# Attention and MoE in one kernel: masks of the first batch on VectorE, more units ahead of batch 1, weights and tokens loaded in another order

## Chip, cores, metric

The kernel runs on one core of one Trainium2 chip. The metric is the device time of one execution in microseconds (us).

In this text TensorE does the matrix multiplications (PE in the profile; PEld is its loading of weights), VectorE is DVE, ScalarE is ACT, GpSimd is POOL, and SyncE is SP, which here issues most DMAs. "Landed" means that a DMA's data has arrived.

## The reference

```python
# 8 batches, 8 heads, 576 tokens, 64 columns a head
scores = q @ k.T / sqrt(64) - slope[h] * (i - j)        # kept where 0 <= i - j < 128
attn   = softmax(scores) @ v
x = attn.transpose(0, 2, 1, 3).reshape(4608, 512)
h = x @ w_in                                            # w_in: 512 x 2048
g = h * clip(h + 3, 0, 6) / 6
out = g @ w_out                                         # w_out: 2048 x 512, out: 4608 x 512 float32
```

## The kernel before

A *group* is two heads of one batch; there are 32 of them, and group 4 opens batch 1, group 8 batch 2. Each group needs its scores (diagonal blocks in `pd`, off-diagonal ones in `po`), exponentials on ScalarE, masks on GpSimd, and the values (`av`), divided on VectorE to `avs`. The MoE part is cut into *units* of four matmuls of 128x512, and `fill(n)` puts n units where TensorE would otherwise wait. A unit needs finished batches, so there is none to put in during batch 0.

Batches 0 and 1 transpose q and k on TensorE. From batch 2 on, q and k are loaded token by token into `ldbuf`, cast by GpSimd into the one buffer `tbuf`, and transposed from there by a DMA into `qTb` and `kTb`. There is one `tbuf`, so each cast waits for the transposing DMA ahead of it. Each engine takes its instructions in the order of the program: in GpSimd's timeline below, the masks of group 9 start at 99.0 us, right behind the cast that began at 96.2.

```python
def load_weights_out():                    # 4 loads of 512 KB, issued by GpSimd
    for g in range(4):
        nc.gpsimd.dma_start(out=w_out_sb[:, ts(g, 4), :], in_=moe_w_out[...])

def load_tokens(b, nm):                    # 5 loads, issued by SyncE
    t = next_ld()[...]
    for j in range(NQ):
        nc.sync.dma_start(out=t[:n, j, :, :], in_=src_of[nm][b, ...])

def cast_tokens(b, nm):                    # q, k: GpSimd to tbuf; v: GpSimd to vbuf
    ...
def xbar(b, nm):                           # the transposing DMA, issued by SyncE
    nc.sync.dma_start_transpose(out=dst, in_=tbuf)

def exp_off(g, e):
    nc.scalar.activation(out=po[:, e], in_=sc[:, e, :], func=ACT.Exp, ...)
    nc.scalar.activation(out=p4[:, e, 0:64], ...)
    nc.gpsimd.affine_select(out=po[:, e], in_=po[:, e], ...)     # mask
    ...
def values(g, qts):                        # called with (0, 1, 2), then with (3, 4)
    av = ps_av.tile([128, 3, 2, W], FP32, tag="av", name="av")   # one PSUM buffer
    ...

def stage_next(g):                         # at the end of group g
    b, hp = divmod(g, NP)                  # NP = 4
    if g == 0:
        new_runs(1); load_runs(1, slice(0, H)); load_tokens(1, "v")
    if g == 1:
        load_weights_out()
    if b == 1:
        if hp == 1:
            load_tokens(2, "v")
        if hp in (1, 2):
            xbar(2, "qk"[hp - 1])
        if hp < 3:
            cast_tokens(2, "qkv"[hp])
    if b >= 2 and b + 1 < B:
        if hp < 2:
            xbar(b + 1, "qk"[hp])
        if hp in (0, 2):
            cast_tokens(b + 1, "kkv"[hp])
    if b >= 1 and b + 2 < B:
        if hp > 0:
            load_tokens(b + 2, "qkv"[hp - 1])
        if hp == 3:
            cast_tokens(b + 2, "q")

# main
...; load_weights_in(); first_batch()
load_tokens(2, "q"); load_tokens(2, "k")
prepare(NP); transposes(NP); prepare(NP + 1)
fill(3)
segment(NP, G, lambda g: (1, 0, 1, 0, 1, 0, 0) if g < 2 * NP else (1, 1, 1, 1, 1, 1, 2))
```

The softmax here doesn't subtract the row's maximum and nothing guards it: scores larger than these inputs give would overflow.

## Time and profile before

| | before |
|---|---|
| median time of the first three runs | 373.83 us (373.61 to 375.56) |
| span of the profiled run | 373.4 us |
| TensorE busy | 315.8 us, 85% |
| TensorE busy from 140 to 300 us | 155.3 of 160 us |
| start of scores of group 4 (batch 1) / of group 8 (batch 2) | 46.2 / 83.1 us |
| start of the cast to `tbuf` of q of batch 2 / of k of batch 3 | 54.9 / 96.2 us |
| start of values of group 9 | 104.1 us |
| from there to the end of the span | 269.3 us |

First, from the page of the kernel before, its rows of 40 equal slices of the span (9.3 us each): busy tenths of TensorE, its granted clock in tenths, busy tenths of the DMA engines, and the bandwidth.

```profile
PE   1456765666998699979999999999999999999995
PEclk9999996969999989999999999999999999999999
DMA  9999997999399959995998999531131010010012
GB/s 158 195 198 192 196 215 117 187 221 198 85 202 202 212 94 222 206 222 127 237 208 181 203 211 226 116 99 46 48 62 49 29 58 28 28 58 28 28 58 84
```

TensorE is short of work mainly in the first ten slices, and DMA is nearly full for the first 25, with three dips. So it is mainly the opening that can move the total, and two things can decide it there: TensorE's own order, or the chain of loads, casts and transposing DMAs.

The next fence is GpSimd's timeline of the kernel before: start, duration, engine, line, operation, output and input; in brackets, how long the engine had been idle and what ended it. The first line is the cast of q of batch 2, the second that of k of batch 2, the third that of k of batch 3, and the last the masks of group 9.

```profile
54.93 2.84 POOL L156 CAST tbuf<-ldbuf 128x512 bf16<-128x512 f32 x5
...
73.05 2.84 POOL L156 CAST tbuf<-ldbuf 128x512 bf16<-128x512 f32 x5 [7.70 <-issue]
...
96.22 2.83 POOL L156 CAST tbuf<-ldbuf 128x512 bf16<-128x512 f32 x5 [6.86 <-DMA qTb<-tbuf]
99.01 1.21 POOL L218 TENSOR_SCALAR_AFFINE_SELECT pd<-pd 128x512 bf16<-128x512 bf16 x2
```

The cast of k of batch 3 waits for the transposing DMA of q of batch 3, and the masks of group 9 stand behind that cast. TensorE's timeline has the scores of groups 4 and 8, and the values of group 9:

```profile
46.19 0.40 PE L195 MATMUL scd<-qTb,kTb 64*128 64x128 bf16 x8
...
83.08 0.40 PE L195 MATMUL scd<-qTb,kTb 64*128 64x128 bf16 x8
...
104.14 0.23 PE L251 MATMUL av<-vbuf,pd 128*128 128x65 bf16 x2
```

From the start of the cast at 96.2 the chain needs 2.8 us for the cast and 0.6 us for the first mask of group 9, so it would have allowed values of group 9 at 99.6 us. They start at 104.1. In the kernel before, TensorE decides, and the chain has 4.5 us to spare.

SyncE's queue in the kernel before (duration is the time to issue) shows q of batch 2 loading beside w_out, k of batch 2 after it, and the transposing DMA of k:

```profile
32.47 18.66 SPq L106 DMA_DIRECT2D ldbuf<-in_q_dram  x5
51.22 5.52 SPq L106 DMA_DIRECT2D ldbuf<-in_k_dram  x5
...
75.95 3.71 SPq L161 DMA_TRANSPOSE kTb<-tbuf  x1
```

Five loads took 18.7 us beside the weights and 5.5 us without them. The table of stretches gives, for 50 to 60 and 60 to 70 us, the busy time and count of PE, PEld, DVE, ACT and POOL, then the granted clock, the DMA share (it adds up the time of packets and can exceed 1) and GB/s:

```profile
50.00:60.00 10.00, 5.29 (x52) 3.02 (x53) 6.77 (x8) 4.79 (x10) 6.35 (x12) 0.78 1.19 206
60.00:70.00 10.00, 7.17 (x76) 4.15 (x77) 6.08 (x14) 5.79 (x12) 2.95 (x6) 0.88 0.54 101
```

### The profile page before, as it was taken

What the parts mean: (1) busy time and instruction counts of PE and PEld (TensorE: products, weight loads), DVE (VectorE), ACT (ScalarE), POOL (GpSimd) and SP (SyncE); (2) the same over time, 40 slices, a digit from 0 to 9 for tenths busy, and PEclk for the clock granted to TensorE, in tenths of its full rate; (3) what the DMA queues carried; (4) which work ended last, traced back from release to release, by engine and by line L of the source; (5) the groups of instructions that cost most, each with busy time, mean ns of one, the idle gap of its engine ahead of it and who ended that gap; (6) DMA issues with size and microseconds to landing.
All of it is one profiled execution on the core that took longest, in us unless ns stands there. A gap on an engine that the chain in (4) does not pass through costs nothing.

```text
span 373.4 us, 6509 instructions
## 1 busy us (share of the span) xinstructions
PE 315.8 (85%) x2408; PEld 160.3 (43%) x2445; DVE 174.2 (47%) x355; ACT 198.5 (53%) x361; POOL 155.3 (42%) x279
## 2 busy tenths in 40 slices
PE   1456765666998699979999999999999999999995
PEld 0334433333444345544544554455445444444442
DVE  5355456634643244545545544555445534434410
ACT  1733264545773366757776666767666343443401
POOL 7398155195555255626674762663332000000000
PEclk9999996969999989999999999999999999999999
DMA  9999997999399959995998999531131010010012
GB/s 158 195 198 192 196 215 117 187 221 198 85 202 202 212 94 222 206 222 127 237 208 181 203 211 226 116 99 46 48 62 49 29 58 28 28 58 28 28 58 84
DMA packets 153135, 51.64 MB, mean 138 GB/s; under 512 B 141200, under 2 KB 148624, under 8 KB 153104
## 3 DMA queue, kind: packets, MB, share of 16 engines
q1 hardware_dynamic: 145504, 44.54, 61.9%
q0 software_dynamic: 7456, 6.55, 10.8%
q8 instruction: 19, 0.31, 0.4%
q10 hardware_dynamic: 144, 0.13, 0.1%
q14 instruction: 12, 0.10, 0.1%
HBM read 36.70 MB, written 9.44 MB: 124 GB/s over the span
## 4 chain that ended last, share of the span: by engine, by line
PE 62%; DVE 8%; ACT 8%; issue 7%; POOL 7%; DMA 6%; SPq 1%; another core or an unknown queue 0%; POOLq 0%
PE ops L303 28%; PE hps L286 28%; ACT r L290 4%; DVE g L291 3%; DMA ldbuf<-in_v_dram 3%; DMA xT<-avs 3%; POOL pd L218 2%; ACT po L225 2%; PE av L251 2%; PE av L248 2%; PE scd L195 2%; POOL po L230 2%; DVE avs L257 1%; DVE osb L317 1%; PE sco L202 1%
## 5 line engine op out<-in xcount | busy, mean ns | idle before, releaser
L291 DVE SCALAR_TENSOR_TENSOR g<-r,hps 128x512 bf16<-128x512 f32 x144 | 99.1, 688 | 146.5 <-ACT r L290 146.4
L290 ACT ACTIVATE r<-hps,bias 128x512 f32<-128x512 f32 x144 | 99.5, 691 | 118.8 <-PE hps L286 115.4
L286 PE MATMUL hps<-xT,w_in_sb 128*128 128x512 bf16 x552 | 151.5, 390 | 11.0 <-DMA xT<-avs 5.2
L303 PE MATMUL ops<-w_out_sb,g 128*128 128x512 bf16 x563 | 144.0, 380 | 5.6 <-DVE osb L317 3.9
L303 PEld LDWEIGHTS <-g 128*128 128x128 bf16 x576 | 55.7, 98 | 78.0 <-issue 13.9
L286 PEld LDWEIGHTS <-w_in_sb 128*128 128x128 bf16 x576 | 52.5, 100 | 59.9 <-issue 11.4
L218 POOL TENSOR_SCALAR_AFFINE_SELECT pd<-pd 128x512 bf16<-128x512 bf16 x64 | 39.3, 636 | 50.3 <-ACT pd L215 50.3
L156 POOL CAST tbuf<-ldbuf 128x512 bf16<-128x512 f32 (+1 forms) x60 | 34.0, 610 | 43.1 <-issue 36.2
L230 POOL TENSOR_SCALAR_AFFINE_SELECT po<-po 128x512 bf16<-128x512 bf16 x64 | 40.0, 633 | 20.5 <-ACT po L225 17.7
L215 ACT ACTIVATE pd<-scd,bias_d 128x512 bf16<-128x512 f32 x64 | 40.7, 684 | 12.2 <-POOL pd L218 11.2
L225 ACT ACTIVATE po<-sco,bias_o 128x512 bf16<-128x512 f32 x64 | 44.1, 690 | 0.0
L248 PE MATMUL av<-vbuf,po 128*128 128x65 bf16 x256 | 27.1, 203 | 8.2 <-DVE avs L257 6.2
L251 PE MATMUL av<-vbuf,pd 128*128 128x65 bf16 x256 | 27.0, 205 | 7.2 <-POOL pd L218 7.2
L257 DVE TENSOR_TENSOR avs<-av,rc 128x384 bf16<-128x384 f32 x64 | 31.4, 491 | 2.2
L251 PEld LDWEIGHTS <-pd 128*128 128x128 bf16 x256 | 21.2, 104 | 17.6 <-POOL pd L218 8.2
L248 PEld LDWEIGHTS <-po 128*128 128x128 bf16 x256 | 20.8, 104 | 14.4 <-DVE avs L257 9.2
L256 DVE RECIPROCAL rc<-av 128x6 f32<-128x6 f32 x64 | 11.8, 184 | 23.6 <-PE av L251 23.4
L183 PE MATMUL tp<-ident,pr 96*128 96x96 bf16 x96 | 8.8, 255 | 16.1 <-DVE pr L171 10.4
L315 ACT COPY osb<-ops 128x512 f32<-128x512 f32 x18 | 10.5, 585 | 19.3 <-PE ops L303 19.3
L228 ACT ACTIVATE p4buf<-sco,bias_d 128x64 bf16<-128x64 f32 x64 | 20.7, 324 | 0.0
L317 DVE COPY osb<-ops 128x512 f32<-128x512 f32 x17 | 11.6, 684 | 7.4 <-PE ops L303 7.4
L195 PE MATMUL scd<-qTb,kTb 64*128 64x128 bf16 x256 | 13.6, 229 | 1.8 <-DVE kTb L185 1.0
(45 smaller groups left out, 150.1 us busy)
## 6 DMA issues: line engine op xcount, KB each, us to landing
out_dram<-osb SPq DMA_DIRECT2D x35, 256.0 KB, 2.3
ldbuf<-in_v_dram SPq DMA_DIRECT2D x32, 256.0 KB, 4.9
ldbuf<-in_q_dram SPq DMA_DIRECT2D x24, 256.0 KB, 4.7
ldbuf<-in_k_dram SPq DMA_DIRECT2D x24, 256.0 KB, 5.0
w_in_sb<-in_moe_w_in_dram POOLq DMA_DIRECT2D x4, 512.0 KB, 14.0
w_out_sb<-in_moe_w_out_dram POOLq DMA_DIRECT2D x4, 512.0 KB, 16.3
ldbuf<-in_v_dram SPq DMA_DIRECT2D x8, 128.0 KB, 4.7
ldbuf<-in_q_dram SPq DMA_DIRECT2D x6, 128.0 KB, 4.7
```

The lines of the kernel that those rows point to most:

```text
L156: nc.gpsimd.tensor_copy(out=tbuf[:m, :, j, :], in_=s[:m, j, :, :].rearrange("p (i e) d -> p i (e d)", e=2))
L215: nc.scalar.activation(out=pd[:, e, :, :].rearrange("p j c -> p (j c)"), in_=sc[:, e, :], func=ACT.Exp, bias=bias_d[:, h:h + 1], scale=scale)
L218: nc.gpsimd.affine_select(out=pd[:, e, :, :], in_=pd[:, e, :, :], pattern=[[0, 4], [1, 128]], channel_multiplier=-1, base=0, compare_op=AL ...
L225: nc.scalar.activation(out=po[:, e, :, :].rearrange("p j c -> p (j c)"), in_=sc[:, e, :], func=ACT.Exp, bias=bias_o[:, h:h + 1], scale=scale)
L230: nc.gpsimd.affine_select(out=po[:, e, :, :], in_=po[:, e, :, :], pattern=[[0, 4], [-1, 128]], channel_multiplier=1, base=-1, compare_op=A ...
L248: nc.tensor.matmul(av[:, i, e, :], lhsT=po[:, e, qt - 1, :], rhs=vb[:, qt - 1, h, :], start=True, stop=False)
L251: nc.tensor.matmul(av[:, i, e, :], lhsT=d, rhs=vb[:, qt, h, :], start=(qt == 0), stop=True)
L257: nc.vector.tensor_tensor(out=st[g, "avs"][:, qts[0]:qts[0] + nq, :, :], in0=av[:, 0:nq, :, 0:D], in1=rc[:, 0:nq, :, :].to_broadcast([128, ...
L286: nc.tensor.matmul(hps, lhsT=w_in_sb[:, ks, ts(ms, 128)], rhs=xT[:, ks, ts(nt, NT)], start=(ks == 0), stop=(ks == n_ks - 1))
L290: nc.scalar.activation(out=r6, in_=hps, func=ACT.Relu, bias=bias3[:, 0:1], scale=1.0 / 6.0)
L291: nc.vector.scalar_tensor_tensor(out=gts[nt][:, ms, :], in0=r6, scalar=1.0, in1=hps, op0=ALU.min, op1=ALU.mult)
L303: nc.tensor.matmul(ops[nt, sub], lhsT=gts[nt][:, ms, ts(sub, 128)], rhs=w_out_sb[:, ms, :], start=(ms == 0), stop=(ms == n_ms - 1))
```

## The change

It is meant to take work off GpSimd and waits out of batch 0, to fill TensorE between batches 0 and 1, and to keep w_out and the tokens of batch 2 from competing with what batches 0 and 1 need first. Its core, with cuts:

```diff
     def prepare(g):
-        for nm in "qk":
+        for nm, eng in (("q", nc.vector), ("k", nc.gpsimd if 2 <= g < NP else nc.vector)):
...
-        cast_v(b, hs, nc.gpsimd)                  # v of batches 0, 1: now cast whole
     def exp_off(g, e):
-        nc.gpsimd.affine_select(out=po[:, e, :, :], ...)
+        if g < NP:
+            nc.vector.tensor_tensor(out=po[:, e, :, :], in0=po[:, e, :, :],
+                                    in1=mask_off.to_broadcast([128, 4, 128]), op=ALU.mult)
+        else:
+            nc.gpsimd.affine_select(out=po[:, e, :, :], ...)
     def values(g, qts):
+        if g < NP and qts[0] > 0:
+            av = ps_h.tile([128, 3, 2, W], FP32, tag="h", name="avh", ...)
+        else:
+            av = ps_av.tile([128, 3, 2, W], FP32, tag="av", name="av")
     def stage_next(g):
         if g == 0:
-            new_runs(1)
+            load_weights_in(2, 4)                 # second half of w_in
+        if g == 1:
             load_runs(1, slice(0, H))
-            load_tokens(1, "v")
-        if g == 1:
-            load_weights_out()
         if b == 1:
+            if hp == 0:
+                cast_tokens(1, "v")
             if hp == 1:
+                cast_tokens(2, "q")
+                xbar(2, "q")
+            if hp == 2:
+                cast_tokens(2, "k")
+                xbar(2, "k")
                 load_tokens(2, "v")
-            if hp in (1, 2):
-                xbar(2, "qk"[hp - 1])
-            if hp < 3:
-                cast_tokens(2, "qkv"[hp])
+                load_weights_out()
+            if hp == 3:
+                cast_tokens(2, "v")
# main
+        load_tokens(1, "v")
         load_tokens(2, "q")
         load_tokens(2, "k")
+        fill(10)
         prepare(NP)
         transposes(NP)
         prepare(NP + 1)
-        fill(3)
-        segment(NP, G, lambda g: (1, 0, 1, 0, 1, 0, 0) if g < 2 * NP else (1, 1, 1, 1, 1, 1, 2))
+        segment(NP, G, lambda g: (1, 0, (g + 1) % 2, 0, 0, 0, 0) if g < 2 * NP else (1, 1, 1, 1, 1, 1, 2))
```

The diff also pins each load to a fixed `ldbuf`, loads only half of w_in ahead of batch 0, and has ScalarE instead of VectorE copy the transposed values of batch 0 (and differently chosen copies of k).

More of the change, by code (lines that the diff above doesn't have):

```diff
@@ L78 @@
     vbuf = [held.tile([128, NQ, H, W], BF16, name=f"vbuf{i}") for i in range(2)]
+    mask_off = held.tile([128, 1, 128], BF16, name="mask_off")
     p4buf = [held.tile([128, 2, 128], BF16, name=f"p4buf{i}") for i in range(2)]
@@ L81, with slot_of @@
     kTb = [held.tile([128, NP, NQ, 128], BF16, name=f"kTb{i}") for i in range(2)]
-    ld, nld = {}, [0]
+    ld = {}
     src_of = {"q": q, "k": k, "v": v}
-    def next_ld():
-        nld[0] += 1
-        return ldbuf[(nld[0] - 1) % 4]
+    def slot_of(b, nm):
+        if nm != "v" and b < 2:
+            return 2 * b
+        if b < 2:
+            return 1 - b
+        return (1, 3, 2, 0)[(3 * (b - 2) + "qkv".index(nm)) % 4]
     def new_runs(b):
-        t = next_ld()[:, :].bitcast(BF16)
+        t = ldbuf[slot_of(b, "q")][:, :].bitcast(BF16)
         for n, nm in enumerate("qk"):
@@ L101, in load_tokens @@
     def load_tokens(b, nm):
-        t = next_ld()[:, 0:NQ * H * D].rearrange("p (j h d) -> p j h d", j=NQ, h=H)
+        t = ldbuf[slot_of(b, nm)][:, 0:NQ * H * D].rearrange("p (j h d) -> p j h d", j=NQ, h=H)
         ld[b, nm] = t
@@ L114, in constants @@
         nc.gpsimd.iota(rel_i, pattern=[[0, 1]], base=0, channel_multiplier=1)
+        nc.gpsimd.memset(mask_off, 1.0)
+        nc.gpsimd.affine_select(out=mask_off, in_=mask_off, pattern=[[0, 1], [-1, 128]],
+                                channel_multiplier=1, base=-1,
+                                compare_op=ALU.is_ge, fill=0.0)
         for i in range(2):
@@ L126, in constants, with load_weights_in @@
                                     scalar2=slopes[h], op0=ALU.add, op1=ALU.mult)
-    def load_weights_in():
-        for g in range(4):
+    def load_weights_in(lo, hi):
+        for g in range(lo, hi):
             nc.gpsimd.dma_start(
@@ L168, in prepare @@
         hs = slice(2 * hp, 2 * hp + 2)
-        for nm in "qk":
+        for nm, eng in (("q", nc.vector), ("k", nc.gpsimd if 2 <= g < NP else nc.vector)):
             pr = prs.tile([RP, RT, 2, D], BF16, tag=f"pr{nm}", name="pr")
-            nc.vector.tensor_copy(
+            eng.tensor_copy(
                 out=pr.rearrange("p t e d -> p e t d"),
@@ L183, in transposes @@
                 nc.tensor.transpose(tp[:, t, :], src[:, t, :], ident[:RP, :RP])
-            eng = nc.scalar.copy if nm == "k" and g % 2 == 0 else nc.vector.tensor_copy
+            eng = nc.scalar.copy if nm == "k" and (g == 0 or g > NP) else nc.vector.tensor_copy
             eng(out=dst[:, hp, :, :].rearrange("p j c -> p (j c)")[:, 0:S].rearrange(
@@ L229, in exp_off @@
                              bias=bias_d[:, h:h + 1], scale=scale)
-        nc.gpsimd.affine_select(out=po[:, e, :, :], in_=po[:, e, :, :],
-                                pattern=[[0, 4], [-1, 128]], channel_multiplier=1, base=-1,
-                                compare_op=ALU.is_ge, fill=0.0)
+        if g < NP:
+            nc.vector.tensor_tensor(out=po[:, e, :, :], in0=po[:, e, :, :],
+                                    in1=mask_off.to_broadcast([128, 4, 128]), op=ALU.mult)
+        else:
+            nc.gpsimd.affine_select(out=po[:, e, :, :], in_=po[:, e, :, :],
+                                    pattern=[[0, 4], [-1, 128]], channel_multiplier=1, base=-1,
+                                    compare_op=ALU.is_ge, fill=0.0)
         if e == 1:
@@ L241, in values @@
         pd, po, p4 = st[g, "pd"], st[g, "po"], p4buf[g % 2]
-        av = ps_av.tile([128, 3, 2, W], FP32, tag="av", name="av")
+        if g < NP and qts[0] > 0:
+            av = ps_h.tile([128, 3, 2, W], FP32, tag="h", name="avh", padded_shape=[128, 3, 2, 85])
+        else:
+            av = ps_av.tile([128, 3, 2, W], FP32, tag="av", name="av")
         nq = len(qts)
@@ L276, in back @@
             nc.tensor.transpose(tp[:, ts(j, 128)], avs[:, j, :], ident)
-        nc.vector.tensor_copy(out=xT[:, hp, ds(b * S, S)], in_=tp[:, 0:S])
+        eng = nc.scalar.copy if b == 0 else nc.vector.tensor_copy
+        eng(out=xT[:, hp, ds(b * S, S)], in_=tp[:, 0:S])
     gts, ops = {}, {}
@@ L368, in first_batch @@
     def first_batch():
-        prepare(0)
         transposes(0)
@@ L438 @@
             load_runs(0, slice(2 * hp, 2 * hp + 2))
-        load_weights_in()
+        load_weights_in(0, 2)
+        prepare(0)
+        cast_tokens(0, "v")
+        new_runs(1)
         first_batch()
+        load_tokens(1, "v")
         load_tokens(2, "q")
         load_tokens(2, "k")
+        fill(10)
         prepare(NP)
```

## The prediction

> **What bounds the kernel now.** The page gives TensorE 315.8 of 373.4 us. The table of stretches puts the idle time early: TensorE is busy 93.6 of the first 140 us, 97% from 140 to 300 us. So only the start can move the total: the time at which batches 0 and 1 are done, plus a TensorE-bound rest. By the timeline, batch 0 ends at 39 us, scores of group 4 (batch 1) start at 46.2, of group 8 (batch 2) at 83.1. DMA is nearly full, about 200 GB/s.
>
> **What the change does.**
> 1. Batch 0: eight 128x512 off-diagonal masks (0.61 us each on GpSimd) go to VectorE, I estimate 0.3-0.6 us; a second PSUM bank removes values' waits on the division (list of waits: about 0.9 us each). But the mask multiplies stand ahead of the divisions in VectorE's order and wait for the exponentials, so a group still takes about 5.5 us (before 4.8-6.7). k's copy of groups 2 and 3 now stands on GpSimd behind the cast of v, whose last piece lands at 17.9 us. The Trainium skill ("SBUF - State Buffer", "Who interferes with whom") says that a VectorE instruction with two SBUF inputs contends with GpSimd's reads; the trace has the kindred case, pr copies of 0.35 us lasting up to 3.2 us beside GpSimd. Gain: 0 to 2 us.
> 2. Ten units instead of three ahead of batch 1. Two PSUM buffers pace them at 1.25 us (TensorE alone 0.87, cold 1.7), so scores of group 4 slip to about 55 us. Batch 1 then carries 6 units, not 12, and shrinks from 37 to 28-30 us. Net about zero.
> 3. Loads. q and k of batch 2 land by about 52 us, but their casts come one group later (behind groups 5 and 6), at about 69 and 77 us. w_out and v of batch 2 queue behind those casts: DMA has a hole of 15-20 us after about 52 us (3 to 4 MB) that the kernel before filled with them. Then both compete; before, token loads beside weight loads got about 65 GB/s (q of batch 2: 18.7 us to issue, others 4.4-5.7).
>
> **On the critical path.** From the cast of q of batch 2 to the transposed q of batch 3 about 8.8 MB must move: at 200-215 GB/s 41-44 us, as before (55 to 96 us). Starting at 69 us it ends near 113, and the cast of k of batch 3 and the masks of group 9, behind it in GpSimd's order, near 119; before, values of group 9 started at 104.1. GpSimd also waits for v of batch 2 before the masks of group 8. This costs up to 14 us, of which later waits return 2-4. If batch 0 and the ten units run faster than I think, most of it vanishes.
>
> **Prediction: 382 us**, 366 to 392 (8 in 10). Faster by over 2%: 0.24; within 2%: 0.27; slower by over 2%: 0.49.
>
> **What would show it.** Timeline: batch 0 ending at 37-40 us; scores of group 4 at 53-57, of group 8 at 83-88. Sliced DMA row: a dip between about 52 and 70 us. Waits: GpSimd's cast of v of batch 2 waiting for its load at 90-100 us, the cast to tbuf for the transposing DMA, values of groups 8 and 9 for GpSimd's masks. From 140 us on TensorE at 95% or more.
>
> **What would make it wrong.** Batch 0 ending near 32 us; units paced at 1 us; batch 1's groups at 5 us or less, with DMA quick enough in the next 30 us: then 362-368 us. TensorE's clock, granted 0.78-0.88 in 50-90 us, may stay full, worth 1-3 us.

## The result, and the profile after

The kernel after took 396.1 us (394.27 to 397.22, four runs), against 373.72 us (373.16 to 375.56) for the kernel before on the same chip: a ratio of 1.058, 95% interval 1.054 to 1.063. Every ratio here is the mean time of one kernel's runs over that of the other's in the same rounds, so it is not quite the ratio of the medians quoted. Executions over 1.5% slower than the fastest of the same kernel are left out of the means. The result is correct in value. The kernel is 5.8% slower, beyond the predicted range.

| us | before | after |
|---|---|---|
| span | 373.4 | 394.0 |
| TensorE busy | 315.8 (85%) | 325.2 (83%) |
| mean granted clock | 0.977 | 0.918 |
| scores of group 4 | 46.2 | 52.2 |
| cast of q of batch 2 to `tbuf` | 54.9 | 69.2 |
| scores of group 8 | 83.1 | 99.2 |
| cast of k of batch 3 starts (q of batch 3 transposed) | 96.2 | 118.9 |
| values of group 9 | 104.1 | 122.4 |
| from values of group 9 to the end | 269.3 | 271.6 |

Of the 20.6 us between the spans, 18.3 lie ahead of the values of group 9. The rows of 40 slices of the kernel after (9.85 us each):

```profile
PE   1557765720787987998999999999999999999986
PEclk9995965675598998999999999999999999999999
DMA  9999800599996996999699899942122101001012
GB/s 175 199 207 205 150 1 2 110 171 198 198 216 131 227 166 146 165 231 197 154 225 212 174 212 217 224 111 62 45 71 45 44 28 53 27 28 53 27 55 80
```

Slices 6 and 7 (49 to 69 us) move 1 and 2 GB/s: the predicted hole. In finer slices it runs from about 47.7 to 73.3 us, 25.6 us in all at 1 GB/s, longer than the predicted 15 to 20. In slice 10 TensorE is hardly busy. Its clock in slices 6 to 11 is 0.5 to 0.7. The same two stretches as before:

```profile
50.00:60.00 10.00, 6.76 (x58) 3.60 (x59) 4.25 (x9) 3.71 (x7) 1.27 (x2) 0.63 0.00 1
60.00:70.00 10.00, 6.61 (x68) 4.43 (x68) 5.00 (x12) 5.08 (x12) 7.83 (x13) 0.50 0.01 2
```

The kernel before moved about 3 MB in these 20 us (206 and 101 GB/s); the kernel after moves almost none. GpSimd's timeline of the kernel after shows the chain that follows. Line numbers are those of the changed kernel: L164 is the cast to `tbuf`, L144 the issue of w_out, L157 the cast of v of batch 2, L225 a diagonal mask.

```profile
69.17 3.09 POOL L164 CAST tbuf<-ldbuf 128x512 bf16<-128x512 f32 x5
...
78.99 2.83 POOL L164 CAST tbuf<-ldbuf 128x512 bf16<-128x512 f32 x5
81.77 3.01 POOL L144 DMA_DIRECT2D w_out_sb<-in_moe_w_out_dram  x4
...
101.46 1.04 POOL L157 CAST vbuf<-ldbuf 128x1024 bf16<-128x1024 f32 x1 [14.04 <-DMA ldbuf<-in_v_dram]
...
118.91 2.83 POOL L164 CAST tbuf<-ldbuf 128x512 bf16<-128x512 f32 x5 [6.61 <-DMA qTb<-tbuf]
121.70 1.21 POOL L225 TENSOR_SCALAR_AFFINE_SELECT pd<-pd 128x512 bf16<-128x512 bf16 x2
```

TensorE's timeline of the kernel after, at the same three points:

```profile
52.17 0.40 PE L202 MATMUL scd<-qTb,kTb 64*128 64x128 bf16 x8 [1.25 <-DVE kTb L192]
...
99.19 0.61 PE L202 MATMUL scd<-qTb,kTb 64*128 64x128 bf16 x8 [15.58 <-DMA kTb<-tbuf]
...
122.38 0.20 PE L265 MATMUL av<-vbuf,pd 128*128 128x65 bf16 x1 [1.06 <-POOL pd L225]
```

Values of group 9 now start 3.5 us after the cast of k of batch 3, which is the cast (2.8) and the first mask (0.6), and the wait that ends just before them is for that mask. So the chain decides, no longer TensorE. The 15.6 us wait ahead of scores of group 8 is the largest single wait of TensorE, and its cause is in SyncE's queue:

```profile
39.17 5.95 SPq L110 DMA_DIRECT2D ldbuf<-in_k_dram  x5
72.28 3.19 SPq L169 DMA_TRANSPOSE qTb<-tbuf  x1
...
81.85 6.74 SPq L169 DMA_TRANSPOSE kTb<-tbuf  x1
88.70 12.21 SPq L110 DMA_DIRECT2D ldbuf<-in_v_dram  x5
```

The transposing DMA of k of batch 2 is issued at 81.85 us, in the same moment as the 2 MB of w_out. The view of DMA issues (last number: us from issue to landing) gives it, first in the kernel before,

```profile
kTb<-tbuf SPq DMA_TRANSPOSE x1, 5.4
```

and in the kernel after:

```profile
kTb<-tbuf SPq DMA_TRANSPOSE x1, 17.3
```

Batch 0 did gain: the last transposes of its values start at 34.0 us instead of 38.95. Its eight masks on VectorE, in the view of their line (shortest/median/longest in ns, first and last start in us):

```profile
L238 DVE TENSOR_TENSOR po<-po,mask_off x8: 414/424/1555, 13.2 to 30.5; 128x512 bf16<-128x512 bf16 x8
```

The Trainium skill ("SBUF — State Buffer", "Who interferes with whom") says that a VectorE instruction with two inputs in SBUF contends with GpSimd's reads and that the loser is blocked completely. The trace agrees with that: seven of the masks take about 0.42 us, and one takes 1.56 us while GpSimd is at work.

### The profile page after: what moved, and what is told of

Read it like the earlier page. It is cut to its first block, busy times and chain, and to the rows that moved or that the text cites. A ratio compares the mean times of both kernels' runs of the same rounds, so it can differ in the third digit from the quotient of the medians.

```text
span 394.0 us, 6536 instructions
## 1 busy us (share of the span) xinstructions
PE 325.2 (83%) x2445; PEld 163.0 (41%) x2445; DVE 174.1 (44%) x357; ACT 201.4 (51%) x365; POOL 152.1 (39%) x265
## 4 chain that ended last, share of the span: by engine, by line
PE 62%; DVE 8%; POOL 8%; ACT 7%; issue 6%; DMA 4%; SPq 4%; POOLq 0%
PE hps L301 27%; PE ops L318 27%; ACT r L305 4%; SPq L110 3%; DMA xT<-avs 3%; DVE g L306 3%; PE scd L202 2%; POOL pd L225 2%; PE av L265 2%; DVE avs L271 2%; POOL tbuf L164 2%; PE av L262 2%; ACT po L232 1%; DMA ldbuf<-in_k_dram 1%; POOL ldbuf L101 1%
## 5 line engine op out<-in xcount | busy, mean ns | idle before, releaser
L301 PE MATMUL hps<-xT,w_in_sb 128*128 128x512 bf16 x576 | 157.4, 399 | 7.4 <-DMA xT<-avs 4.7
L318 PE MATMUL ops<-w_out_sb,g 128*128 128x512 bf16 x576 | 146.6, 382 | 4.7 <-DVE osb L332 3.9
L301 PEld LDWEIGHTS <-w_in_sb 128*128 128x128 bf16 x576 | 53.5, 101 | 62.8 <-issue 15.2
L225 POOL TENSOR_SCALAR_AFFINE_SELECT pd<-pd 128x512 bf16<-128x512 bf16 x64 | 39.5, 637 | 77.0 <-ACT pd L222 76.9
L164 POOL CAST tbuf<-ldbuf 128x512 bf16<-128x512 f32 (+1 forms) x60 | 34.2, 615 | 34.2 <-issue 27.6
L241 POOL TENSOR_SCALAR_AFFINE_SELECT po<-po 128x512 bf16<-128x512 bf16 x56 | 35.4, 639 | 22.0 <-ACT po L232 19.4
L271 DVE TENSOR_TENSOR avs<-av,rc 128x384 bf16<-128x384 f32 (+1 forms) x60 | 29.7, 495 | 2.1
L262 PE MATMUL av<-vbuf,po 128*128 128x65 bf16 x240 | 25.0, 202 | 5.4 <-DVE avs L271 3.8
L202 PE MATMUL scd<-qTb,kTb 64*128 64x128 bf16 x256 | 14.0, 235 | 18.4 <-DMA kTb<-tbuf 15.6
L265 PE MATMUL av<-vbuf,pd 128*128 128x65 bf16 x248 | 25.5, 204 | 1.8 <-POOL pd L225 1.8
L262 PEld LDWEIGHTS <-po 128*128 128x128 bf16 x256 | 21.1, 105 | 10.1 <-DVE avs L271 5.0
L270 DVE RECIPROCAL rc<-av 128x6 f32<-128x6 f32 (+1 forms) x60 | 11.0, 183 | 31.7 <-PE av L265 31.7
L157 POOL CAST vbuf<-ldbuf 128x1024 bf16<-128x1024 f32 x16 | 16.4, 1050 | 16.9 <-DMA ldbuf<-in_v_dram 16.9
L202 PEld LDWEIGHTS <-kTb 64*128 64x128 bf16 x256 | 7.9, 100 | 30.4 <-DMA kTb<-tbuf 15.8
## 6 DMA issues: line engine op xcount, KB each, us to landing
w_in_sb<-in_moe_w_in_dram POOLq DMA_DIRECT2D x4, 512.0 KB, 10.1
```

Source lines behind the costliest of these rows:

```text
L164: nc.gpsimd.tensor_copy(out=tbuf[:m, :, j, :], in_=s[:m, j, :, :].rearrange("p (i e) d -> p i (e d)", e=2))
L225: nc.gpsimd.affine_select(out=pd[:, e, :, :], in_=pd[:, e, :, :], pattern=[[0, 4], [1, 128]], channel_multiplier=-1, base=0, compare_op=AL ...
L241: nc.gpsimd.affine_select(out=po[:, e, :, :], in_=po[:, e, :, :], pattern=[[0, 4], [-1, 128]], channel_multiplier=1, base=-1, compare_op=A ...
L262: nc.tensor.matmul(av[:, i, e, :], lhsT=po[:, e, qt - 1, :], rhs=vb[:, qt - 1, h, :], start=True, stop=False)
L265: nc.tensor.matmul(av[:, i, e, :], lhsT=d, rhs=vb[:, qt, h, :], start=(qt == 0), stop=True)
L271: nc.vector.tensor_tensor(out=st[g, "avs"][:, qts[0]:qts[0] + nq, :, :], in0=av[:, 0:nq, :, 0:D], in1=rc[:, 0:nq, :, :].to_broadcast([128, ...
```

## The experiments

Three theories; the expectations call them by number:

- **Theory 1, the chain.** The casts of q and k of batch 2 come late, DMA idles, and w_out and the tokens must then all pass ahead of q of batch 3. That delays the masks of group 9, and with them the total.
- **Theory 2, TensorE's wait.** The loss is the 15.6 us that TensorE waits for k of batch 2, whose transposing DMA shares the engines with w_out. Take the wait away and the time returns.
- **Theory 3, the ten units.** The loss is the ten units ahead of batch 1, with TensorE's low granted clock in batch 1. Put three there again and all of the time returns; move w_out and none does.

Two numbers were read in every run: the start of the cast of k of batch 3 (*chain*), and the start of values of group 9. Where they lie about 3.5 us apart, the chain decides; where clearly further, TensorE does (e7, at 4.4, lies between). The expectations put values of group 9 of the kernel after at 124.1 us; the first of their matmuls starts at 122.4, which is what the table counts. "Before" in the ratios is the kernel before on the same chip.

| run | scores g4 | scores g8 | chain | values g9 | apart | rest of span | median us | ratio (95%) |
|---|---|---|---|---|---|---|---|---|
| before | 46.2 | 83.1 | 96.2 | 104.1 | 7.9 | 269.3 | 373.7 | 1 |
| after | 52.2 | 99.2 | 118.9 | 122.4 | 3.5 | 271.6 | 396.1 | 1.058 (1.054–1.063) |
| e1 | 52.0 | 86.7 | 107.7 | 111.2 | 3.5 | 271.8 | 383.3 | 1.025 (1.020–1.030) |
| e2 | 51.9 | 88.4 | 118.0 | 121.6 | 3.6 | 270.6 | 393.9 | 1.052 (1.048–1.056) |
| e3 | 42.9 | 89.4 | 108.8 | 112.3 | 3.5 | 273.6 | 385.7 | 1.028 (1.022–1.035) |
| e4 | 44.0 | 82.9 | 107.4 | 110.9 | 3.5 | 272.9 | 386.3 | 1.033 (1.028–1.037) |
| e5 | 42.8 | 78.8 | 92.4 | 100.9 | 8.5 | 269.6 | 371.7 | 0.989 (0.984–0.994) |
| e6 | 42.4 | 74.7 | 95.8 | 99.3 | 3.5 | 272.0 | 374.5 | 0.996 (0.992–1.001) |
| e7 | 42.0 | 71.9 | 97.1 | 101.5 | 4.4 | 269.7 | 372.2 | 0.990 (0.985–0.995) |
| e8 | 43.5 | 72.7 | 87.2 | 94.0 | 6.8 | 272.1 | 367.1 | 0.983 (0.978–0.987) |
| e9 | 53.1 | 86.3 | 101.5 | 107.7 | 6.2 | 269.7 | 379.5 | 1.010 (1.005–1.015) |
| e10 | 52.5 | 82.1 | 94.7 | 102.5 | 7.8 | 269.5 | 372.5 | 0.996 (0.990–1.002) |
| e11 | 52.0 | 80.5 | 94.3 | 102.0 | 7.7 | 272.6 | 378.0 | 1.014 (1.010–1.018) |

The rest of the span lies between 269.3 and 273.6 us in all thirteen, while values of group 9 start anywhere from 94.0 to 122.4. So the start of values of group 9 carries most of every large difference, with up to some 4 us from the rest; differences below that (e7 against e6, e11 against e10) cannot be read from it alone. The starts are those of one profiled run each; a repeat of batch 0 can shift them by about 2 us.

### e1: w_out at the end of batch 0

```diff
# from the kernel after
             if hp == 2:
...
-                load_weights_out()
# main
         load_tokens(2, "k")
+        load_weights_out()
         fill(10)
```

> The changed kernel (396.1 us, values of group 9 at 124.1 us), with w_out issued at the end of batch 0, about 31 us, so that it moves in the hole of the DMA (46 to 72 us). Theory 1 (the casts of batch 2 come late, and all the loads queued behind them, w_out among them, are a volume of DMA that delays the masks of group 9): 2.1 MB less behind the casts is 10 to 11 us at 200 GB/s, so values of group 9 at about 112 us and the total at 384 to 386. Theory 2 (only the weight load beside the transposing DMA of k does harm, by its 15.6 us wait of TensorE): the wait is gone, values of group 9 near 105, total 372 to 377. Theory 3 (ten units ahead and TensorE's low clock in batch 1): 392 or more.

Measured: 383.3 us, so 12.8 of the 22.4 us came back with w_out loading into the hole. Values of group 9 moved from 122.4 to 111.2. GpSimd's timeline of e1 still has the chain waiting for q of batch 3:

```profile
107.70 2.84 POOL L164 CAST tbuf<-ldbuf 128x512 bf16<-128x512 f32 x5 [7.13 <-DMA qTb<-tbuf]
```

That is close to what theory 1 asked for (384 to 386), and not what theory 2 (372 to 377) or theory 3 (392 or more) did. The casts of batch 2 are as late as in the kernel after (68.9 against 69.2), and that part of the loss stays.

### e2: w_out behind the transposing DMA of k

```diff
# from the kernel after
             if hp == 2:
...
-                load_weights_out()
             if hp == 3:
+                load_weights_out()
                 cast_tokens(2, "v")
```

> The changed kernel with w_out issued one group later, behind the transposing DMA of k of batch 2 but still ahead of v of batch 2 being cast. Both theories: k's transposing DMA lands in about 5 us again (near 87 us) and TensorE's wait of 15.6 us for it is gone. Theory 1 (volume): the same bytes stand before the transposed q of batch 3, so values of group 9 stay at 118 to 124 us and the total at 391 to 396. Theory 2 (that wait is the loss): 378 to 383.

Measured: 393.9 us. The transposing DMA of k now landed in 7.7 us instead of 17.3. In TensorE's timeline of e2, the scores of group 8, the values of group 8 and the values of group 9:

```profile
88.40 0.61 PE L202 MATMUL scd<-qTb,kTb 64*128 64x128 bf16 x8 [5.97 <-DMA kTb<-tbuf]
...
109.40 0.23 PE L265 MATMUL av<-vbuf,pd 128*128 128x65 bf16 x1 [9.92 <-POOL pd L225]
...
121.57 0.19 PE L265 MATMUL av<-vbuf,pd 128*128 128x65 bf16 x1
```

TensorE's wait shrank from 15.6 to 6.0 us, and scores of group 8 came 10.8 us earlier, yet values of group 9 came only 0.8 us earlier. A new wait of 9.9 us stands ahead of values of group 8, for GpSimd's masks. The volume ahead of q of batch 3 had not changed, and v of batch 2 now took 16.9 us to issue beside w_out. Most of the wait was taken away and about 2 us of 22 came back, so theory 2 falls: the largest wait of TensorE in the profile was not the loss.

### e3: three units ahead of batch 1, not ten

```diff
# from the kernel after
-        fill(10)
         prepare(NP)
         transposes(NP)
         prepare(NP + 1)
-        segment(NP, G, lambda g: (1, 0, (g + 1) % 2, 0, 0, 0, 0) if g < 2 * NP else ...)
+        fill(3)
+        segment(NP, G, lambda g: (1, 0, 1, 0, 1, 0, 0) if g < 2 * NP else ...)
```

> The changed kernel with three units after the first transposes of batch 1 and three in each of its groups, as before, instead of ten ahead and six. Theory 1: scores of group 4 at about 42 us, cast of q of batch 2 at about 60 instead of 69, everything behind it 8 to 10 us earlier, total 386 to 389. Theory 2: 394 to 397. Theory 3 (ten units ahead and the low clock are the loss): 373 to 378.

Measured: 385.7 us; 10.4 us came back. GpSimd's timeline of e3, the casts of q of batch 2 and of k of batch 3:

```profile
59.57 3.08 POOL L164 CAST tbuf<-ldbuf 128x512 bf16<-128x512 f32 x5
...
108.80 2.83 POOL L164 CAST tbuf<-ldbuf 128x512 bf16<-128x512 f32 x5 [6.39 <-DMA qTb<-tbuf]
```

Batch 1 started 9.3 us earlier, the cast of q of batch 2 came 9.6 us earlier (69.2 to 59.6), and the end of the chain 10.1 us earlier (118.9 to 108.8). The chain passed the shift on almost one to one. The ten units did not only cost TensorE's time: they pushed the casts, and with them the loads, to a later time. Theory 2 had expected nothing back (394 to 397): TensorE still waits 16.2 us for k of batch 2 in e3, and its transposing DMA takes 18.6 us. Theory 3 had expected everything back (373 to 378), so it falls as the whole cause.

### e4: in the kernel before, w_out late and nothing else

```diff
# from the kernel before
-        if g == 1:
-            load_weights_out()
         if b == 1:
+            if hp == 2:
+                load_weights_out()
```

> The kernel before with w_out issued at group 6, behind the cast of k of batch 2 (its place in the changed kernel), and nothing else changed. Theory 1: DMA moves 2.1 MB more behind the casts and less ahead of them, about 10 us late less 3 to 5 us of slack: 378 to 382. Theory 2: k's transposing DMA is slowed beside it as in the changed kernel, scores of group 8 8 to 12 us late: 382 to 386. Theory 3: 373 to 375.

Measured: 386.3 us, more than theory 1's 378 to 382 and at the end of theory 2's 382 to 386; but theory 2 wanted scores of group 8 to be 8 to 12 us late, and they start at 82.9 us instead of 83.1. SyncE's queue and GpSimd's timeline of e4:

```profile
78.02 17.20 SPq L106 DMA_DIRECT2D ldbuf<-in_k_dram  x5
```

```profile
107.41 2.83 POOL L156 CAST tbuf<-ldbuf 128x512 bf16<-128x512 f32 x5 [17.37 <-DMA qTb<-tbuf]
```

Here k of batch 3 got the slow place beside w_out, and the chain ended 11.2 us later (96.2 to 107.4). About 4.5 us of that had been slack, so values of group 9 moved by 6.8, and the rest of the span grew by another 3.6. TensorE's wait for k of batch 2 is 2.0 us here (its transposing DMA took 8.8 us). So moving w_out behind the tokens of batch 2 suffices to lose some 3%, with little wait for k of batch 2. Batch 0 of this profiled run happened to end 2.0 us earlier than in the kernel before, so counted from the cast of q of batch 2 (52.7 us, before 54.9) the chain became 13.4 us longer. The size was missed because the expectation allowed too much slack and nothing later.

### e5: in the kernel before, VectorE's masks and the second PSUM bank alone

```diff
# from the kernel before
+        if g < NP:
+            nc.vector.tensor_tensor(out=po[:, e, :, :], in0=po[:, e, :, :],
+                                    in1=mask_off.to_broadcast([128, 4, 128]), op=ALU.mult)
+        else:
             nc.gpsimd.affine_select(out=po[:, e, :, :], ...)
...
+        if g < NP and qts[0] > 0:
+            av = ps_h.tile([128, 3, 2, W], FP32, tag="h", name="avh", ...)
+        else:
             av = ps_av.tile(...)
```

> The kernel before with only the first batch's off-diagonal masks on VectorE and the second PSUM bank for the second half of the values. Batch 0 should end about 4 us earlier, near 35 us (it did in the changed kernel). If only TensorE's work at the start counts, the total falls by those 4 us, to 369 to 370.5. Theory 1 (the chain of loads and casts of batches 2 and 3 decides when the masks of group 9 are done, and it starts when q of batch 2 lands, which the DMA decides): most of the 4 us is lost again, 371 to 374.

Measured: 371.7 us, ratio 0.989. Values of group 9 came 3.2 us earlier and the total fell by 1.1%, 3.8 us in the medians (375.5 on that chip to 371.7). Theory 1 had expected most of batch 0's gain to be lost to the chain. The 371.7 us lie in its range of 371 to 374 only because the kernel before took 375.5 on that chip; as a difference it was wrong. The chain did not stay where it was: the cast of q of batch 2 came 3.4 us earlier (54.9 to 51.5) and the end of the chain 3.8 us earlier (96.2 to 92.4), so it kept its slack and TensorE's gain came through. This part of the change is good by itself.

### e6: both repairs at once

```diff
# from the kernel after: the edits of e1 and e3 together
```

> The changed kernel with both: w_out at the end of batch 0 (which gave back 12.8 us alone) and three units ahead (10.4 us alone). Theory 1: both act on the same chain, one by its volume, one by its start, and they add as far as the chain still decides: cast of q of batch 2 at 60 us, transposed q of batch 3 by 97 to 99, values of group 9 at 103 to 105, total 372 to 375. If they were the same loss counted twice, 380 to 383.

Measured: 374.5 us. The 21.6 us that came back (by medians, as for the two alone) are close to the sum of the two alone (12.8 + 10.4 = 23.2). The chain still decides (3.5 us apart), because the casts of batch 2 still follow groups 5 and 6, at 58.0 us instead of the kernel before's 54.9, though batch 1 begins earlier than before. The sum of the two repairs brings the loss back to nothing, within the interval. But e6 still holds batch 0's gain, which e5 puts at 1.1%, so its later casts may still cost about that much; e7 tests them.

### e7: the casts one group earlier as well

```diff
# from e6
             if hp == 0:
                 cast_tokens(1, "v")
-            if hp == 1:
                 cast_tokens(2, "q")
                 xbar(2, "q")
-            if hp == 2:
+            if hp == 1:
                 cast_tokens(2, "k")
                 xbar(2, "k")
                 load_tokens(2, "v")
-            if hp == 3:
+            if hp == 2:
                 cast_tokens(2, "v")
```

> The run before this (w_out at the end of batch 0, three units ahead) with the casts and transposing DMAs of q and k of batch 2 and its v one group earlier, as in the kernel before. Theory 1: cast of q of batch 2 at 54 to 57 us, transposed q of batch 3 by about 93, so that TensorE itself decides: values of group 9 at 98 to 102 us, total 366 to 371, which would beat both kernels. If the chain was no longer what decided, the same as the run before this.

Measured: 372.2 us, a miss against 366 to 371. The cast of q of batch 2 came 5.5 us earlier (52.6), but the end of the chain did not (97.1). In the list of waits of TensorE in e7 (in total, times, longest):

```profile
PE av L265 <- POOL pd L225: 6.5, 2, 6.2
```

Values of group 7 waited 6.2 us for GpSimd's masks, since the cast of v of batch 2, now a group earlier too, made GpSimd wait for that load until 79.3 us. An early place in an engine's order is worth nothing when its data is not there.

### e8: v of batch 2 and q of batch 3 ahead of others

```diff
# from e7
             if hp == 1:
                 cast_tokens(2, "k")
-                xbar(2, "k")
                 load_tokens(2, "v")
+                xbar(2, "k")
...
-            if hp < 2:
+            if hp < 2 and g != 2 * NP:
                 xbar(b + 1, "qk"[hp])
...
+            if g == 2 * NP - 1:
+                cast_tokens(b + 2, "q")
+                xbar(b + 2, "q")              # ahead of the load of v of batch 3
             if hp > 0:
                 load_tokens(b + 2, "qkv"[hp - 1])
-            if hp == 3:
+            if hp == 3 and g != 2 * NP - 1:
                 cast_tokens(b + 2, "q")
```

> The kernel with w_out at the end of batch 0, three units ahead and the casts a group earlier (372.2 us), in which GpSimd still waited for v of batch 2 until 79.3 us (TensorE's values of group 7 6.2 us for the masks behind it) and for the transposed q of batch 3 until 97 us. Here the loads of v of batch 2 are issued ahead of k's transposing DMA, and q of batch 3 is transposed ahead of the load of its v. Theory 1 (this chain decides): the wait of values of group 7 goes, the cast of k of batch 3 ends by about 90 us, values of group 9 start at 93 to 98 us, total 363 to 368. If TensorE or the later loads decide already: 370 to 372.

Measured: 367.1 us (365.8 to 369.6, six runs) against 374.2 us before (ten runs): ratio 0.983, interval 0.978 to 0.987. It beats both kernels; that it is 2% or more below the kernel before is not shown. GpSimd's and TensorE's timelines of e8:

```profile
87.22 2.83 POOL L164 CAST tbuf<-ldbuf 128x512 bf16<-128x512 f32 x5 [4.05 <-DMA qTb<-tbuf]
```

```profile
94.04 0.23 PE L265 MATMUL av<-vbuf,pd 128*128 128x65 bf16 x2
```

The chain ends at 87.2 and would allow the values at about 90.7; they start at 94.0. TensorE decides again, 10.1 us earlier than in the kernel before. Of these, 7.3 us arrive in the span, since the rest of it is 2.8 us longer.

### e9: in the kernel before, ten units ahead and nothing else

```diff
# from the kernel before
+        fill(10)
         prepare(NP); transposes(NP); prepare(NP + 1)
-        fill(3)
-        segment(NP, G, lambda g: (1, 0, 1, 0, 1, 0, 0) if g < 2 * NP else ...)
+        segment(NP, G, lambda g: (1, 0, (g + 1) % 2, 0, 0, 0, 0) if g < 2 * NP else ...)
```

> The kernel before with only the units moved: ten ahead of batch 1, six in it. Scores of group 4 at about 55 instead of 46 us. Theory 1: the cast of q of batch 2 stands behind the masks of group 4 and moves from 55 to about 63 us, all loads that follow it likewise, so values of group 9 near 110 us instead of 104 and a total of 378 to 382. Moving units alone, without that chain: equal work, 372 to 375, or 1 to 3 us more by the lower clock.

Measured: 379.5 us, which is inside 378 to 382, but for a partly wrong reason. The ratio on the same chip is only 1.010, and the chain does not decide (6.2 us apart). TensorE itself arrives later: scores of group 4 start 6.9 us later, and batch 1 is only 3.7 us shorter (33.2 against 36.9 us from scores of group 4 to scores of group 8). So the loss here is that the moved units are not returned in full. Batch 0 of this profiled run ended 2.4 us earlier than in the kernel before (last transposes at 36.5 instead of 38.95); counted from its end, scores of group 4 start 9.4 us later.

### e10: e8 with ten units ahead

```diff
# from e8: the same edit as in e9
```

> The run before this with ten units ahead of batch 1 and six in it. Theory 1: the casts of batch 2 start 8 to 10 us later, behind group 4's masks at about 60 us, so 4 to 9 us slower than the run before this: 369 to 375. If ten units ahead are harmless once the loads are in order: within 2 us of it.

Measured: 372.5 us over five runs, 5.4 more than e8 by the medians, in the same rounds on the same chip. That is inside theory 1's 369 to 375, but not for its reason: the chain is not the limit (7.8 us apart). TensorE's timelines have the scores of groups 4 and 8, first of e8, then of e10:

```profile
43.52 0.40 PE L202 MATMUL scd<-qTb,kTb 64*128 64x128 bf16 x8
...
72.68 0.40 PE L202 MATMUL scd<-qTb,kTb 64*128 64x128 bf16 x8
```

```profile
52.45 0.40 PE L202 MATMUL scd<-qTb,kTb 64*128 64x128 bf16 x8 [1.25 <-DVE kTb L192]
...
82.05 0.61 PE L202 MATMUL scd<-qTb,kTb 64*128 64x128 bf16 x8
```

Scores of group 4 start 8.9 us later, and batch 1 takes 29.6 us with six units against 29.2 us with twelve in e8. The six units less inside batch 1 shortened it by nothing. It follows that in e8 they stood in time in which batch 1 waits anyway.

### e11: e10 with TensorE kept busy

One suspicion was left: in e10 and in the kernel after, TensorE's granted clock is low in batch 1. The Trainium skill ("TensorE: Matmul & The Clock Gate", "What's actually happening") says that the clock is set by how busy the engine has been shortly before, half when it was idle. The traces agree in kind: in the kernel after TensorE was busy for 6.6 of the 10 us from 60 to 70 us and 0.50 was granted; in e11, below, it was busy for 8.3 of them and 1.00 was granted. e11 adds matmuls whose result nobody reads, so the outcome stays correct.

```diff
# from e10
+    def keep_busy(g, n):                     # 4 + 4 + 3 in each group of batch 1
+        if NP <= g < 2 * NP:
+            wm = ps_o.tile([128, NT], FP32, tag="o", name="wm")
+            for _ in range(n):
+                nc.tensor.matmul(wm, lhsT=w_in_sb[:, 0, 0:128], rhs=xT[:, 0, 0:NT],
+                                 start=True, stop=True)
```

> The run with ten units ahead on top of the reordered loads (e10, 373.1 us; e8, with three, 367.1), plus 44 matmuls of 128x512 in batch 1 whose result nobody reads, 11 in each group, placed where TensorE waits. They are extra work, 0.22 us each at the full clock (9.5 us of busy time in all), and change nothing else; the outputs stay right. If the 6 us that ten units cost come from TensorE's low granted clock in batch 1 (0.50 to 0.76 in 60-80 us, units taking 1.89 instead of 1.04 us), the clock stays near 1 and the total falls to 367 to 370.5 in spite of the extra work. If they come from the order of the work and its waits, the extra work can only cost: 373 to 380.

Measured: 378.0 us, ratio 1.014. The tables of stretches (clock is the third number from the end), e10 first, then e11:

```profile
60.00:70.00 10.00, 7.35 (x68) 4.54 (x65) 3.98 (x9) 4.06 (x8) 8.41 (x15) 0.50 0.34 65
70.00:80.00 10.00, 6.08 (x71) 4.08 (x70) 4.61 (x11) 6.33 (x12) 7.98 (x13) 0.76 1.10 204
```

```profile
60.00:70.00 10.00, 8.33 (x98) 4.92 (x97) 6.83 (x12) 5.85 (x12) 9.53 (x16) 1.00 0.23 44
70.00:80.00 10.00, 9.07 (x95) 5.02 (x95) 5.23 (x13) 6.89 (x14) 8.07 (x14) 1.00 1.21 210
```

The clock was full from 60 to 80 us, batch 1 took 28.5 us instead of 29.6, and values of group 9 came only 0.5 us earlier (102.0 against 102.5). That speaks against the low clock as a cause of the slow batch 1 in e10. It doesn't measure the clock's worth alone, because the added matmuls also take TensorE's time. The rest of the span grew by 3.1 us, and no run here says why. The profiled run of e11 (376.3 us) was also its fastest; by the ratios (1.014 against 0.996) the loss is larger than these two traces show.

## Why the prediction was wrong

The direction, for which 0.49 had been given, and the mechanism of the third step were right; the size was not. The predicted time was 382 us with 392 as the upper end, and 396.1 us was measured.

What failed is the sum under "On the critical path". Its term "at 200-215 GB/s 41-44 us" measured 49.7 us, and where it had "later waits return 2-4", a further 2.3 us were lost. "Net about zero" in step 2 failed as well; but the shift that it denied stands in the prediction's own path, as the cast of q at 69 us, and so is not what separates 382 from 396.

**Batch 0 (step 1): too low.** A gain of 0 to 2 us and an end at 37 to 40 us were predicted. The last transposes start at 34.0 us instead of 38.95. Part of it is no merit of the change: the last piece of v landed at 13.8 us instead of the 17.9 that the prediction took over, but with an unchanged batch 0 it landed at 15.9 and 15.4 in e4 and e9, and their last transposes started at 36.9 and 36.5. e5 shows that VectorE's masks and the second bank alone are worth about 4 us of the total. The masks' 0.42 us lie in the estimated 0.3 to 0.6.

**Ten units ahead (step 2): this step failed in its "net about zero".** The pace and the shift were about right: the ten units run from 34.75 to 48.4 us, 1.37 us each against 1.25 predicted, and scores of group 4 start at 52.2, a little ahead of the range of 53 to 57 because batch 0 ended earlier. What failed is the assumption that batch 1 shrinks when six units leave it. e10 against e8 shows it plainly: 29.6 us with six units, 29.2 with twelve, and 5.4 us lost by the medians. In e9 3.7 of 6.9 us came back. In the change itself batch 1 took 47.0 us, 15.6 of them the wait for k of batch 2, instead of the predicted 28 to 30; and the later batch 1 also delayed the casts: e3 gives 10.4 us for the ten units.

**The loads (step 3): right mechanism, mis-sized terms.** The hole in DMA (1 to 2 GB/s from 50 to 70 us), the cast of q of batch 2 at 69.2 us (predicted 69, partly by luck: scores of group 4 came 3 us earlier than the 55 assumed, and the cast followed 17 us behind them instead of 14), the cast of k at 79.0 (predicted 77), the wait of GpSimd for v of batch 2 and the limit at the masks of group 9 are all in the trace. e1, e3, e4 and e6 support the chain as the cause. From the cast of q of batch 2 to the cast of k of batch 3 the tables of stretches give, first in the kernel before and then in the kernel after:

```profile
54.90:96.20 41.30, 26.64 (x253) 14.93 (x259) 22.20 (x41) 22.33 (x42) 22.53 (x41) 0.83 0.97 182
```

```profile
69.20:118.90 49.70, 26.11 (x225) 13.95 (x223) 16.92 (x35) 19.55 (x37) 22.22 (x38) 0.69 1.06 178
```

Three terms were wrong in size:

- *"At 200-215 GB/s 41-44 us".* From 69.2 to 118.9 us the trace has 49.7 us at 178 GB/s, which is 8.8 MB: the volume was right and the rate wrong. DMA moved next to nothing until 73.3 us, the first transposing DMA being issued at 72.3, and from there it averaged 195 GB/s. The kernel before held a warning: its own stretch from 54.9 to 96.2 us averaged 182 GB/s, so it moved 7.5 MB there. "As before" was true of the time but not of the volume, and 8.8 MB at 182 GB/s take 48 us. The chain then ends at 118.9 instead of 113, and values of group 9 start at 122.4 instead of 119.
- *Scores of group 8 at 83 to 88 us.* They started at 99.2, because the transposing DMA of k took 17.3 us beside w_out instead of 5.4. The prediction had priced that competition for token loads only. e2 shows that this error in itself cost only about 2 us of the total, which is not clear of the noise.
- *"Later waits return 2-4."* They returned nothing: the rest of the span grew by 2.3 us.

**The sum.** 373.8 + 14 - (2 to 4) gives 384 to 386 by the prediction's own terms, and 382 was written. The number lies below its own sum, for which the text gives only the hedge that most of the loss vanishes if batch 0 and the ten units run faster. Batch 0 did end earlier than predicted (34.0 us), and the loss did not vanish: the cast of q still came at 69.2. With the chain's real lateness of 18.3 us at values of group 9 plus 2.3 us of the rest, the sum is the measured difference of the spans, 20.6 us (the medians differ by 22.4; the profiled run of the kernel before was itself 1.4 us above its median).

What stays open: from the kernel before, w_out late (3.3%) and ten units ahead (1.0%), less the gain of e5 (1.1%), make up about 3% of the 5.8%. The rest may come from what they do together, since each alone has the slack of 4.5 us to use up first, and from the casts one group later, which no run tested in the kernel before; that is not shown. Also, how the DMA engines divide their time between the weight load and the other queue was seen in durations only, and why the rest of the span varies by some 4 us was not tested.

## What to carry to other kernels

Follow the loads back to the instruction that lets them start: here a cast moved one group later, and ten units ahead of it, left the DMA engines idle for 25 us, and the bytes saved from the crowded start met the critical transposing DMAs later. Put large weight loads where the DMA queue would be idle, and before moving work out of a stage, check that the stage is limited by that work: six units fewer did not shorten batch 1 in e10, and in e9 gave back only part of what the move had cost. The largest wait in a profile is not the loss if something else arrives just as late: measure the slack of the second chain (here 4.5 us) before you price a change.

## What the Trainium skill lacked or had wrong

- "DMA: Bandwidth & Descriptors", section "Issuing engines are not separate DMA queues", says that DMAs of all issuing engines run on the same 16 engines and interleave. The traces agree with that, but the page gives no figure for what a small DMA loses. Here a transposing DMA took 17.3 us beside 2 MB of weights that GpSimd had issued, against 5.4 us with only token loads around it, and five token loads took 16.9 to 18.7 us to issue (e2, e4 and the kernel before) instead of 5.5.
- "TensorE: Matmul & The Clock Gate" explains the low clock, but has no word on what it costs in a stage whose pace TensorE does not set. Here it was granted at 0.50 for stretches of 10 us and a unit took 1.89 us instead of 1.04 us; yet restoring the clock by extra matmuls (e11), whose own time is in the figure, moved the deciding point by 0.5 us only.
- "GPSIMD Engine Reference", section "4.1 Engine selection", calls elementwise work with one input on GpSimd roughly line-rate, and names a factor against VectorE for two inputs only. A learner could take the two engines as equal for a copy. The copy of k of two heads (96x768, bf16 to bf16, one input) took 0.81 to 1.0 us on GpSimd and mostly 0.35 to 0.39 us on VectorE (up to 3.2 us where it ran beside GpSimd's own work).
